# Batch 0's output products of a retention layer: one float32 matmul a head in place of three float16 ones

## The chip, the cores and the metric

The kernel runs on one core of a Trainium2 chip. The metric is the device time of one execution in microseconds (us); smaller is better. A core has a matrix engine (TensorE, PE in the profile, with its weight loads listed apart as PEld), three engines for elementwise work (VectorE or DVE, ScalarE or ACT, GpSimd or POOL), and SyncE (SP), which issues most DMAs here.

## The reference

Retention with a decay per head over blocks of tokens, then a Fourier mixing layer with an MLP, then a second MLP layer. What matters for the change is the retention, cut to its core (B = 2, H = 8 heads, S = 768 tokens, D = 64):

```python
intra = np.einsum('bhic,bhjc->bhij', qb, kb) * Dmask[None]     # masked scores
intra = np.einsum('bhij,bhjd->bhid', intra, vb)                # output products
inter = np.einsum('bhid,bhde->bhie', qb * lam_pow[None], kv_state)
out[:, :, sl] = intra + inter
kv_state = lam_block[None, :, None, None] * kv_state + np.einsum('bhsd,bhse->bhde', kb_dec, vb)
```

Behind it follow `X = fft2(x)`, `u = x + real(X)`, a layer norm, `relu(un @ w_ch1) @ w_ch2`, and the same norm and MLP once more with other weights. The reference computes in float32.

## The kernel before

**Tiling.** The kernel takes blocks of 128 tokens instead of 64, so each batch has 6 blocks (c = 0 to 5). A block of q, k or v for all 8 heads is a tile of 128 x 512 float32 (256 KB). Heads are worked in two sets, even and odd (e = 0, 1), of 4 heads each.

**Precision.** Much of the kernel splits a float32 value into a float16 pair, a high part and a remainder, and makes a product as three float16 matmuls (high by high, high by remainder, remainder by high; `PASS` in the code). In batch 0 some products multiply float32 tiles directly: scores, interstate products and the Fourier products. In the trace each float32 matmul stands as two records of a weight load and a matmul.

**One block of the retention** (batch 0), in the order in which its data flow:
- `attn_a`: GpSimd scales the keys by their decay (line 322); ScalarE and VectorE make the float16 pairs of values (lines 326, 327) and keys (lines 331, 332).
- `attn_scores` (line 346): 8 float32 matmuls, k by q, into two PSUM banks.
- `attn_x` (lines 353 to 358), once for each head set: VectorE multiplies the scores by the decay mask and a constant into `m32`, ScalarE rounds that to float16, GpSimd takes the remainder.
- `attn_o_steps` (line 426): for each of 8 heads three float16 matmuls, weights 128x128 (masked scores) and 64 moving columns (values); then VectorE adds the interstate part and writes the block to its place in `U` (lines 430, 432). For some blocks ScalarE also copies one row (lines 436 to 443).
- `attn_s_steps`: the state, 24 float16 matmuls (line 458), VectorE's sum with the decayed old state (line 465), and ScalarE's copy of it into a block-diagonal tile (line 470).
- `attn_i_steps` (line 375): the interstate product of the next block, 4 float32 matmuls from that tile, and VectorE's scaling of it (line 379).

**Order.** A scheduler orders the instructions of blocks 0 to 4 on each engine from estimated times. The end of the stage (outputs and state of block 4, all of block 5) and the Fourier stage behind it stand in an order written by hand, `ORDER`, for PE, VectorE, GpSimd and ScalarE. Its first line is

```python
c0 S B1 B0 s s B1 B0 s s O4 B1 B0 O4 c0 I O4 R I O5 O5 O5 O5 c0 c1 c2 W12 k2 j2 ...
```

where each word is the next step of a chain: S the scores of block 5, B1 and B0 the steps of `attn_x` for its two head sets, s the state of block 4, O4 and O5 outputs, I the interstate product of block 5, c0 to c2 weight conversions, W12 twelve dummy matmuls, k2 and j2 the first folds of the Fourier stage (line 489). Behind the Fourier stage come the MLPs of both layers (matmuls at lines 698, 708, 801, 848), between which the retention of batch 1 runs.

**Loads.** SyncE issues all loads of batch 0's q, k and v first, in order of blocks; tables and weights follow.

Of the kernel before, what the change touches and what calls it, by code (L numbers as in the profile page):

```python
# [15 lines left out]
ALU = mybir.AluOpType  # L16
# [16 lines left out]
QS = 64.0  # L33
MS = 256.0
# [90 lines left out]
def tile_retention_fourier_mlp(ctx: ExitStack, tc: tile.TileContext, a: dict, out: bass.AP):  # L125
    nc = tc.nc
    pe, act, dve, pool, sp = nc.tensor, nc.scalar, nc.vector, nc.gpsimd, nc.sync
# [18 lines left out]
    def bank(which, name):  # L146
        return banks[which].tile([P, 512], F32, tag=which, name=name)

    def f32t(name, spare=None):
        if spare is not None:  # L150
            return wpool.tile([P, 512], F32, tag=f"w2_{spare}", name=name)
        return fp.tile([P, 512], F32, tag="f", name=name)

    def hl(name):
        return fp.tile([P, 2, 512], F16, tag="f", name=name)
# [17 lines left out]
    loaded = {}  # L173
# [89 lines left out]
    def run(steps):  # L263
        for t in steps:
            pass
        return t
# [46 lines left out]
    vs, ks, ms = {}, {}, {}  # L313
# [34 lines left out]
    def attn_x(b, c, e, bk):  # L348
        m32 = f32t(f"m32_{b}_{c}_{e}")
        mk = mask[:, e::2]  # L350
        mk = mk[:, :, :P] if c >= 3 else mk[:, :, P:0:-1]
        mo, mi = (z.rearrange("p (h i) -> p h i", i=P) for z in (m32, pss[e]))
        dve.scalar_tensor_tensor(mo, mi, MS, mk, op0=ALU.mult, op1=ALU.mult)
        yield
        t = ms[b, c, e] = hl(f"m{b}_{c}_{e}")
        act.copy(t[:, 0], m32)
        yield
        pool.tensor_tensor(t[:, 1], m32, t[:, 0], op=ALU.subtract)  # L358
        yield

    def attn_b(b, c, bk):
        steps = [attn_x(b, c, e, bk) for e in range(2)]
        attn_scores(b, c, bk)
        for z in steps:
            next(z)
        for z in steps:
            run(z)
# [36 lines left out]
    def row_fold(b):  # L404
        y_ = row0[b]
        r = f32t(f"r{b}", 5 if b == 0 else None)
        c_ = f32t(f"rc{b}", 14 if b == 0 else None)
        pool.tensor_tensor(c_[0:1, 1:256], y_[0:1, 1:256], y_[0:1, 511:256:-1], op=ALU.add)
        pool.tensor_copy(c_[0:1, 0:257:256], y_[0:1, 0:257:256])
        pool.tensor_tensor(r[0:1, :P], c_[0:1, :P], c_[0:1, 256:128:-1], op=ALU.subtract)  # L410
        pool.tensor_tensor(r[0:1, P:ND], c_[0:1, :P + 1], c_[0:1, 256:127:-1], op=ALU.add)
        yield
        t = f32t(f"rhl{b}", 6 if b == 0 else None).bitcast(F16)[0:1].rearrange("p (two n) -> p two n", two=2)[:, :, :ND]
        act.copy(t[:, 0], r[0:1, :ND])
        yield
        pool.tensor_tensor(t[:, 1], r[0:1, :ND], t[:, 0], op=ALU.subtract)
        rhl[b] = t
        yield

    def attn_o_steps(b, c, bk):  # L420
        ps = bank(bk["o"], f"ps_o{b}_{c}")
        for h in range(H):
            (i, e), hc = divmod(h, 2), slice(h * D, (h + 1) * D)
            m_, mc = ms[b, c, e], slice(i * P, (i + 1) * P)
            for n, (x, y) in enumerate(PASS):
                pe.matmul(ps[:, hc], m_[:, x, mc], vs[b, c][:, y, hc], start=n == 0, stop=n == 2)
        yield
        x_ = U[b][c] if c < 3 else U[b][8 - c]
        if c == 0:
            dve.tensor_scalar(x_, ps, XS, None, op0=ALU.mult)  # L430
        else:
            dve.scalar_tensor_tensor(x_, ps, XS, xt[b, c], op0=ALU.mult, op1=ALU.add)
        yield
        if c == 3:
            row0[b] = f32t(f"row0{b}", 4 if b == 0 else None)
            act.copy(row0[b][0:1], x_[0:1])
            if b > 0:
                run(row_fold(b))
        elif c > 3:
            act.copy(U[b][9 - c][0:1], x_[0:1])  # L440
        yield
        if c == NCH - 1:
            act.copy(x_[0:1], row0[b][0:1])
        yield
# [28 lines left out]
    def attn_c(b, c, bk):  # L473
        run(attn_o_steps(b, c, bk))
        if c < NCH - 1:
            run(attn_s_steps(b, c, bk))
# [451 lines left out]
    def eng(n):  # L928
        return pool if n in ONPOOL.split() else dve

    wide = {}
    chains = {"s": lambda: attn_s_steps(0, 4, bk0), "O4": lambda: attn_o_steps(0, 4, bk0),
              "O5": lambda: attn_o_steps(0, 5, bk0), "I": lambda: attn_i_steps(0, 5, bk0), "R": lambda: row_fold(0)}
    for x in range(2):
        chains[f"B{x}"] = lambda x=x: attn_x(0, 5, x, bk0)
# [19 lines left out]
    with tc.manual_schedule(engines={mybir.EngineType.PE, mybir.EngineType.DVE, mybir.EngineType.Pool, mybir.EngineType.Activation}):  # L955
        for z in ORDER.split():
# [3 lines left out]
            if z[0] == "W":  # L960
                ps = bank("up", f"warm{len(warm)}")
# [145 lines left out]
```

## Time and profile before

| What | us |
|---|---|
| time, median of 3 runs | 605.07 |
| lowest and highest | 604.65, 605.29 |
| the profiled execution, its own time | 605.77 |
| span of the profiled execution | 603.9 |
| PE, busy in the span | 576.7 |
| VectorE, busy | 416.1 |
| GpSimd, busy | 280.0 |
| ScalarE, busy | 262.8 |

The profile is one execution, with the start and duration of each instruction. A busy PE isn't PE at its peak: its matmuls are pipelined and their recorded durations overlap. What a row of a pipelined burst costs is read from the whole burst and its count, not from the duration of one. Idle time of an engine is shown with what ended it. [...]

### The profile page before, as it was taken

Reading aid. Unit: us, or ns where it says so; the run is one execution under the profiler, and the core shown is the slowest. Engines: PE = TensorE matmul, PEld = TensorE weight load, DVE = VectorE, ACT = ScalarE, POOL = GpSimd, SP = SyncE. Lnnn points to the kernel's source line nnn. Section 1 sums busy time; section 2 is a strip of 40 time slices with the busy share of each in tenths; the row PEclk is TensorE's granted clock in tenths of the full one; section 3 lists DMA queues with packets and bytes.
Section 4 is the critical chain, followed back from the end, with each engine's and each line's share of the span. In section 5 each row is a group of like instructions: output and inputs, shape, how many; then the busy total and the mean of one; then the engine's idle time right before and its main releaser. Section 6 shows DMA issues by size and latency. Waiting matters only on the chain.

```text
span 603.9 us, 11882 instructions
## 1 busy us (share of the span) xinstructions
PE 576.7 (95%) x4669; PEld 379.3 (63%) x4669; DVE 416.1 (69%) x905; ACT 262.8 (44%) x530; POOL 280.0 (46%) x294
## 2 busy tenths in 40 slices
PE   6879899999999998999988999999999999999997
PEld 3756646565644554676756677666677777767773
DVE  5998799884794698886697679867544553555333
ACT  3654689654223433453457675753222222221110
POOL 7854789986253666342349665963011200020000
PEclk9899999999999999999998999999999999999999
DMA  8995259962000100443163652510110027102001
GB/s 278 396 400 187 71 176 295 304 205 69 1 1 1 35 19 9 107 130 105 46 194 111 189 162 79 158 27 1 61 28 18 2 79 63 18 1 84 22 2 52
DMA packets 46326, 63.23 MB, mean 105 GB/s; under 512 B 26176, under 2 KB 28350, under 8 KB 46270
## 3 DMA queue, kind: packets, MB, share of 16 engines
q1 hardware_dynamic: 45598, 62.40, 34.4%
q8 instruction: 36, 0.59, 0.4%
q10 hardware_dynamic: 672, 0.08, 0.1%
q14 instruction: 20, 0.16, 0.1%
HBM read 52.23 MB, written 6.29 MB: 97 GB/s over the span
## 4 chain that ended last, share of the span: by engine, by line
PE 62%; DVE 19%; ACT 7%; POOL 6%; issue 4%; DMA 1%; SPq 0%; DVEq 0%; POOLq 0%; ACTq 0%
PE ps_y L848 30%; PE ps L801 22%; PE ps_h L708 4%; DVE wf L295 2%; DVE bst L642 2%; ACT top L292 2%; DVE ps_w L294 2%; DVE tr L761 2%; PE ps_d L518 1%; POOL m L358 1%; POOL w L310 1%; PE ps_s L346 1%; PE ps_i L388 1%; POOL kd L322 1%; ACT w L308 1%
## 5 line engine op out<-in xcount | busy, mean ns | idle before, releaser
L848 PE MATMUL ps_y<-w,h 128*128 128x512 f16 x1152 | 281.9, 380 | 3.5 <-ACT h L833 1.7
L848 PEld LDWEIGHTS <-h 128*128 128x128 f16 x1152 | 109.2, 98 | 102.6 <-ACT h L833 3.8
L801 PEld LDWEIGHTS <-sw 128*128 128x128 f16 x1104 | 94.8, 98 | 23.2 <-issue 7.1
L801 PE MATMUL ps<-th,sw 128*128 128x192 f16 x828 | 92.9, 246 | 5.1 <-DVE s L814 3.6
L801 PEld LDWEIGHTS <-w 128*128 128x128 f16 x828 | 72.6, 99 | 19.1 <-issue 0.8
L310 POOL TENSOR_TENSOR w<-wf,w 128x512 f16<-128x512 f32 x58 | 67.1, 1164 | 36.3 <-ACT w L308 36.2
L833 ACT ACTIVATE h<-ps 128x384 f16<-128x384 f32 x92 | 43.8, 488 | 72.8 <-DVE ps L827 68.4
L708 PE MATMUL ps_h<-unT,w 128*128 128x384 f16 x396 | 73.7, 326 | 1.7 <-DVE h L723 1.6
L801 PE MATMUL ps<-unT,w 128*128 128x192 f16 x552 | 63.6, 248 | 0.0
L834 DVE SCALAR_TENSOR_TENSOR h<-ps,h 128x384 f16<-128x384 f32 x92 | 49.5, 554 | 14.2 <-ACT h L833 12.6
L708 PEld LDWEIGHTS <-w 128*128 128x128 f16 x396 | 36.9, 98 | 29.8 <-issue 3.1
L753 POOL TENSOR_TENSOR sw<-ws,sw 128x512 f16<-128x512 f32 x32 | 37.9, 1197 | 33.9 <-ACT sw L752 33.8
L821 DVE TENSOR_TENSOR t<-ps,s 128x192 f32<-128x192 f32 x46 | 16.3, 353 | 50.3 <-PE ps L801 50.0
L292 ACT ACTIVATE top<-ws 128x512 f16<-128x512 bf16 x57 | 44.2, 777 | 10.4 <-DVE wf L295 10.3
L813 ACT COPY s<-ps 128x192 f32<-128x192 f32 x46 | 14.5, 314 | 73.3 <-PE ps L801 73.3
L671 POOL TENSOR_TENSOR uns<-un,uns 128x512 f16<-128x512 f32 x21 | 24.6, 1171 | 43.6 <-ACT uns L670 43.4
L295 DVE TENSOR_TENSOR wf<-ps_w,top 128x512 int32<-128x512 int32 x61 | 41.3, 681 | 2.4 <-POOL w L310 1.2
L777 POOL TENSOR_TENSOR th<-ts,th 128x384 f16<-128x384 f32 x24 | 22.1, 940 | 43.2 <-ACT th L776 43.2
L308 ACT CAST w<-wf 128x512 f16<-128x512 f32 x58 | 34.9, 609 | 10.3 <-DVE wf L295 10.1
L294 DVE TENSOR_SCALAR ps_w<-ws 128x512 int32<-128x512 int32 x55 | 37.8, 689 | 0.9
L827 DVE TENSOR_TENSOR ps<-ps,s 128x192 f32<-128x192 f32 x46 | 16.6, 361 | 28.6 <-PE ps L801 28.4
L814 DVE TENSOR_TENSOR s<-ps,s 128x192 f32<-128x192 f32 x46 | 16.2, 353 | 27.7 <-ACT s L813 27.6
(161 smaller groups left out, 807.2 us busy)
## 6 DMA issues: line engine op xcount, KB each, us to landing
ws<-in_w SPq DMA_DIRECT2D x25, 511.8 KB, 4.8
ws<-in_w2b SPq DMA_DIRECT2D x16, 511.8 KB, 3.5
ws<-in_w1b SPq DMA_DIRECT2D x16, 511.8 KB, 3.6
kt<-in_kt SPq DMA_DIRECT2D x12, 256.0 KB, 4.1
qt<-in_qt SPq DMA_DIRECT2D x12, 256.0 KB, 5.6
v<-in_v SPq DMA_DIRECT2D x12, 256.0 KB
k<-in_k SPq DMA_DIRECT2D x12, 256.0 KB, 5.9
pre<-in_w SPq DMA_DIRECT2D x4, 511.8 KB
```

Of the source, the lines that this page charges most:

```text
L292: act.activation(top[:, :, 1], raw.bitcast(BF16)[:, :, 2], AF.Copy, scale=TOPS)
L294: dve.tensor_scalar(part, raw[:, :, 0], 13, None, op0=ALU.logical_shift_right)
L295: dve.tensor_tensor(ti, part, top.rearrange("p n two -> p (n two)").bitcast(I32), op=ALU.bitwise_or)
L308: act.copy(hi, t)
L310: (dve if m == 0 and i in (LD1 if kind == 1 else LD2) else pool).tensor_tensor(lo, t, hi, op=ALU.subtract)
L671: pool.tensor_tensor(s_[:, 1], un, s_[:, 0], op=ALU.subtract)
L708: pe.matmul(ps, w[:, i, k, fo:fo + P], x[:, j, k, :], start=n == 0, stop=n == 11)
L753: pool.tensor_tensor(lo, z, hi, op=ALU.subtract)
L801: pe.matmul(ps, lhs, rhs, start=start and n == 0, stop=n == 5, skip_group_check=True)
L833: act.activation(hi, z, AF.Relu)
L834: dve.scalar_tensor_tensor(lo, z, 0.0, hi, op0=ALU.max, op1=ALU.subtract)
L848: pe.matmul(dn[blk][j], h[:, x, j * P:(j + 1) * P], w[:, y], start=f == 0 and n == 0, stop=f == NF - 1 and n == 2)
```

## The change

In batch 0 the masked scores stay the float32 tile `m32`; the cast and the remainder (lines 356 and 358) aren't made, and their two steps in `ORDER` are empty. The output product of a head is one matmul of `m32` and the loaded float32 values, in place of three. The scaling of the values, which the float16 pair of the values carries, goes into the mask product's constant. The float16 pairs of values and keys are still made. Batch 1 is as before.

```diff
--- before.py
+++ after.py
@@ -350,8 +350,13 @@
         mk = mask[:, e::2]
         mk = mk[:, :, :P] if c >= 3 else mk[:, :, P:0:-1]
         mo, mi = (z.rearrange("p (h i) -> p h i", i=P) for z in (m32, pss[e]))
-        dve.scalar_tensor_tensor(mo, mi, MS, mk, op0=ALU.mult, op1=ALU.mult)
-        yield
+        dve.scalar_tensor_tensor(mo, mi, MS if b else MS * QS, mk, op0=ALU.mult, op1=ALU.mult)
+        yield
+        if b == 0:
+            ms[b, c, e] = m32
+            yield
+            yield
+            return
         t = ms[b, c, e] = hl(f"m{b}_{c}_{e}")
         act.copy(t[:, 0], m32)
         yield
@@ -422,6 +427,9 @@
         for h in range(H):
             (i, e), hc = divmod(h, 2), slice(h * D, (h + 1) * D)
             m_, mc = ms[b, c, e], slice(i * P, (i + 1) * P)
+            if b == 0:
+                pe.matmul(ps[:, hc], m_[:, mc], loaded["v", b, c][:, hc], start=True, stop=True)
+                continue
             for n, (x, y) in enumerate(PASS):
                 pe.matmul(ps[:, hc], m_[:, x, mc], vs[b, c][:, y, hc], start=n == 0, stop=n == 2)
         yield
```

## Rows read from the trace of the kernel before

**Rows 1.** The page: the span, and each engine's busy time, share and instructions.
```profile
span 603.9 us, 11882 instructions
...
PE 576.7 (95%) x4669; PEld 379.3 (63%) x4669; DVE 416.1 (69%) x905; ACT 262.8 (44%) x530; POOL 280.0 (46%) x294
```

**Rows 2.** Stretches: busy us (x count) of PE, PEld, DVE, ACT, POOL; clock, DMA share, GB/s.
```profile
20.00:30.00 10.00, 8.02 (x142) 6.81 (x138) 9.06 (x15) 6.33 (x13) 7.38 (x7) 1.00 1.04 403
30.00:40.00 10.00, 7.92 (x136) 6.80 (x136) 9.59 (x15) 5.41 (x11) 8.62 (x11) 1.00 1.02 406
...
140.00:604.00 464.00, 450.69 (x3496) 298.30 (x3494) 298.59 (x681) 173.18 (x358) 169.77 (x179) 0.99 0.23 60
```

**Rows 3.** Groups to 60 us: count, busy us, mean ns, idle before, releaser.
```profile
L358 POOL TENSOR_TENSOR m<-m,m 128x512 f16<-128x512 f32 x12 | 15.7, 1325 | 4.1 <-ACT m L356 4.1
...
L426 PE MATMUL ps_o<-vhl,m 128*128 128x64 f16 x144 | 7.3, 201 | 1.9 <-POOL m L358 1.7
...
L356 ACT CAST m<-m 128x512 f16<-128x512 f32 x12 | 7.0, 616 | 3.2 <-DVE m L353 3.2
```

**Rows 4.** Order of time, PE weight loads: start, us, engine, line, operation, count, [idle].
```profile
19.86 0.46 PEld L458 LDWEIGHTS <-khl 128*64 128x64 f16 x22
...
25.06 0.61 PEld L426 LDWEIGHTS <-m 128*128 128x128 f16 x19
25.60 0.97 PEld L375 LDWEIGHTS ps_i<-diag,qt 128*128 128x128 f32 x8
...
118.55 0.96 PEld L388 LDWEIGHTS ps_i<-state,qt 64*128 64x128 f32 x14 [0.23 <-issue]
```

**Rows 5.** PE alone by stretch: us, busy (instructions), granted clock, DMA share, GB/s.
```profile
12.00:13.00 1.00, 1.00 (x21) 0.54 1.06 389
13.00:14.00 1.00, 0.30 (x2) 0.50 1.05 387
14.00:18.00 4.00, 3.74 (x45) 0.50 1.05 387
18.00:19.00 1.00, 1.00 (x22) 0.54 1.07 387
```

**Rows 6.** Order of time, PE matmuls of the first stage.
```profile
14.58 1.20 PE L426 MATMUL ps_o<-vhl,m 128*128 128x64 f16 x19
...
27.85 1.16 PE L346 MATMUL ps_s<-qt,kt 64*128 64x128 f32 x16 [1.09 <-DVE m L353]
...
30.40 0.26 PE L426 MATMUL ps_o<-vhl,m 128*128 128x64 f16 x3 [1.22 <-POOL m L358]
...
34.76 0.73 PE L426 MATMUL ps_o<-vhl,m 128*128 128x64 f16 x19 [0.50 <-POOL m L358]
36.40 1.16 PE L375 MATMUL ps_i<-diag,qt 128*128 128x128 f32 x8 [0.90 <-ACT diag L470]
37.39 0.86 PE L426 MATMUL ps_o<-vhl,m 128*128 128x64 f16 x24
```

**Rows 7.** Order of time, VectorE up to the first fold, and one of ScalarE.
```profile
21.80 1.64 DVE L332 TENSOR_TENSOR khl<-kd,khl 128x512 f16<-128x512 f32 x1
...
25.91 0.69 DVE L327 SCALAR_TENSOR_TENSOR vhl<-v,vhl 128x512 f16<-128x512 f32 x1 [0.94 <-ACT vhl L326]
...
28.64 0.68 DVE L332 TENSOR_TENSOR khl<-kd,khl 128x512 f16<-128x512 f32 x1
...
31.04 1.53 DVE L327 SCALAR_TENSOR_TENSOR vhl<-v,vhl 128x512 f16<-128x512 f32 x1
...
33.10 1.27 DVE L353 SCALAR_TENSOR_TENSOR m<-ps_s,mask 128x512 f32<-128x512 f32 x2
...
34.89 0.41 DVE L465 TENSOR_TENSOR state<-ps_st,dec 128x256 f32<-128x256 f32 x1
...
38.99 0.68 DVE L489 TENSOR_TENSOR e<-u 128x512 f32<-128x512 f32 x1
...
35.53 0.81 ACT L470 COPY diag<-state 64x256 f32<-64x256 f32 x2
```

## The prediction

> **What bounds the kernel now.** I read the page first. TensorE is busy 95% of the span, VectorE 69%, and ScalarE and GpSimd under 50% [rows 1]. That is an average over unlike stages, so the busy times by stretch come next [rows 2]: from 140 us to the end PE is busy 450.7 of 464 us, but in the first 40 us it is not the only full engine. There the first batch's attention runs, the only place the edit touches (the scores of batch 0, lines 353 to 358, and its output products, line 426). From 20 to 40 us VectorE is busy 9.06 and 9.59 of each 10 us, PE 8.02 and 7.92. I then read the instruction groups of this stage by shape for the price of what goes [rows 3], PE's weight loads for the price of what comes [rows 4], the granted clock [rows 5], and the order of time on PE and the other engines up to the first fold [rows 6, 7]. That fold, on VectorE at 38.99 us, is my checkpoint: everything behind it (folds, Fourier products, layer norm, MLP) follows in a fixed order or from a full PE, so I carry a shift of it to the end one for one. DMA doesn't hold that point: it moves 403 and 406 GB/s from 20 to 40 us, but batch 0's q, k, v are 24 loads of 256 KB, 6.3 MB; at that rate from some 5 us on they are in near 21 us, 17 us earlier.
>
> **What is removed.** Twelve casts on ScalarE of 0.616 us and twelve subtractions on GpSimd of 1.325 us: 7.0 us and 15.7 us of busy time [rows 3]. No engine they leave is the bound of the stage, so they pay only where somebody waits for them. PE does: its two visible waits on the GpSimd result are 1.22 and 0.50 us [rows 6], and 1.7 us in all [rows 3]. A second payment is that VectorE loses time beside GpSimd. The key remainder at line 332 took 1.64 us beside two long subtractions and 0.68 us where GpSimd was idle for most of it; the value remainder at line 327 took 1.53 us beside a third, and 0.69 us before that [rows 7]. These two alone are 0.95 + 0.84 = 1.8 us. [...] VectorE's own twelve mask products stay and cost the same: only the constant changes.
>
> **What is added.** Per block, 24 float16 matmuls of 64 columns become 8 float32 ones. Each float32 matmul of this kernel stands as two records: the 4 of line 375 give 8 rows. So 24 rows become 16. What is one row worth? The 128x64 product in float32 with 128 rows of weights isn't in the trace, so I bound it. Float16 at line 426: 19 weight loads in 0.61 us, (0.61 - 0.10)/18 = 0.029 us a row [rows 4]. Float32 at line 375, the same weights with 128 columns: 8 loads in 0.97, (0.97 - 0.19)/7 = 0.112 us. Is that the weights or the 128 columns? Line 388 has 64 columns, in two halves of 64 rows that run side by side: 14 loads in 0.96, seven pairs, (0.96 - 0.19)/6 = 0.128 us a pair, with one uneven pair at the end. Half the columns, no faster: the weight load sets the pace. So I take 0.112; the lower end is the 0.056 us that line 388 gives if its halves had run one after the other. Per block 16 x 0.112 = 1.79 us against 24 x 0.029 = 0.70: **1.09 us more PE per block**, 6.5 us over six blocks (at the lower end 0.90 us a block, 0.2 more). [...]
>
> **The sum along PE.** Block 0 is nearly free: the subtraction kept PE from finishing its product until 15.8 us [rows 6], and PE was busy only 0.30 us of 13 to 14 [rows 5]. In float32 it can start behind the scores of block 1, near 12.3 us, and at the half clock of that stretch takes 2 x 1.79 = 3.6 us, to 15.9: no change. From 15.54 (interstate product of block 1) to 26.57, the last load of block 3's, PE has next to no idle, so blocks 1 and 2 add 2 x 1.09: it gets there at 28.75 instead. What is then left is scores 4 (1.16 less the 0.19 that runs on beside the next burst: 0.97), output 3 (1.79), interstate 4 (0.97), scores 5 (0.97), state 4 (22 loads took 0.46 [rows 4]: 0.5 for 24), output 4 (1.79), interstate 5 (0.97), output 5 (1.79) and a drain of 0.2: 9.95 us, to 38.70. Before, PE ended this at 37.39 + 0.86 = 38.25 after waits of 1.09, 1.22, 0.50 and 0.90 us [rows 6]; these are what pays for three times 1.09. That is +0.45. One wait stays: interstate 5 needs ScalarE's copy of state 4 (0.81 us [rows 7]), behind VectorE's last two mask products (1.27 us) and the state sum (0.41): with 0.2 from PE, 0.2 + 1.27 + 0.41 + 0.81 + gaps of 0.1 = 2.8 us after scores 5, and PE has 0.5 + 1.79 = 2.3 us of work for it. 0.5 more. **The fold starts 0.9 us later.** The GpSimd waits are gone, and PE's own weight loads are late instead. The profiled execution took 605.77 us, 1.87 over its span and 0.70 over the median of the runs, 605.07; on the profiled base the sum gives 606.7, on the median **606.0**.
>
> **The rivals.** (1) *VectorE stays the bound and gains.* If PE finds idle time for the wide products, VectorE sets the fold, without the 1.8 us of collisions and the early waits behind GpSimd (PE's gap at 13 us is one). For it: it is the fuller engine from 20 us on. Against: PE's sum above has no room. It would take a PE row of 0.056 us, or an order that moves outputs 0 and 1 into gaps before 15.5. I price it at the two collisions and half of the 1.72 us waited for GpSimd: -2.7, 602.4. [...]
> (2) *The clock returns sooner.* [...] Float32 rows of block 0 fill the gap before 14.1. If the clock returned at 15.5, the work of 3.4 us at half speed would take 1.7: 606.0 - 1.7 = 604.3. Against: from 14 to 18 us PE was busy 3.74 of 4 us and the clock still stayed at half until the end of it; I see no row that puts the return earlier.
> (3) *Outputs get in front of scores: slower.* PE takes its queue in order. An output of 1.79 us queued ahead of scores 4 or 5 delays the mask products, and with them VectorE, by that much; from the point where VectorE has no other ready work it is paid in full. With outputs 1, 2 and 3 all ahead of scores 5, and of PE's waits only the 1.09 us ahead of scores 4 won back, scores 5 come 3 x 1.09 - 1.09 = 2.2 us later, and the 0.5 us of interstate 5 comes on top: 2.7, 607.8. For it: in the trace outputs 1 and 2 stand ahead of scores 4. Against: output 3 stood behind scores 5, and before interstate 4 PE has a wait of 1.22 us to give.
>
> **How the numbers follow.** About 0.2% (1.2 us) is what a measurement of this kernel can tell from no change. Forecast, PE-bound: 0.38, its own range 604.9 to 607.4. Rival 1: 0.22. Rival 2: 0.15. Rival 3: 0.25. Faster by over 1.2 us: most of rival 1 and a third of rival 2, 0.26. Slower: most of rival 3 and a third of the forecast, 0.36. Same: 0.38. For 8 in 10 the range takes in both far rivals: 602.2 to 608.2. The order of the work behind the first stage is planned from estimates that the edit shifts, and may move a us either way; that is in the range.
>
> **What would show it.** Right: the output product's weight loads 0.11 us apart, 1.8 us a block; PE without waits between 20 and 38 us; the fold at 39.5 to 40.3; VectorE's line 332 and 327 at 0.7 us. A fold near 36 means rival 1; full clock before 18.9, rival 2; scores 4 or 5 starting later than 29 and 32.5 with VectorE idle ahead of its mask products, rival 3. A row of 0.06 us would take the ground from under the forecast, and so would a fold that moves while the end doesn't.

## The result, and the profile after

The change makes the kernel slower. Its median is 610.57 us (608.93 to 613.58, 11 executions) beside 606.07 us for the kernel before on the same chip (604.65 to 609.17, 11 executions): a ratio of 1.0082, 95% interval 1.0064 to 1.0101. The forecast was 606.0 us with a range of 602.2 to 608.2, so the time lies outside it.

The profiled execution took 613.24 us, 7.47 more than the one of before. It is one of the three slowest of the eleven, so its profile shows the loss near its largest; the medians differ by 4.5 us. The page of the kernel after, span and busy times, answers to [rows 1]:

```profile
span 611.5 us, 11759 instructions
...
PE 589.3 (96%) x4621; PEld 391.6 (64%) x4621; DVE 414.8 (68%) x905; ACT 256.6 (42%) x518; POOL 264.2 (43%) x282
```

ScalarE and GpSimd gave up 6.2 and 15.8 us, near the 7.0 and 15.7 of the removal. PE has 48 instructions fewer and 12.6 us more. Where, the stretches of the kernel after show (busy us and count of PE, PEld, DVE, ACT, POOL, then granted clock, DMA share, GB/s):

```profile
10.00:20.00 10.00, 9.87 (x87) 9.02 (x88) 6.56 (x10) 4.14 (x9) 4.47 (x5) 0.50 1.05 387
20.00:30.00 10.00, 10.00 (x75) 9.12 (x75) 5.84 (x10) 2.48 (x5) 1.87 (x3) 0.51 1.04 405
30.00:40.00 10.00, 10.00 (x115) 8.95 (x112) 7.34 (x12) 3.15 (x7) 1.32 (x2) 1.00 1.02 404
```

PE is full from 20 to 40 us, VectorE busy 5.84 and 7.34 us where it was 9.06 and 9.59 [rows 2]. The column behind the busy times is the surprise: the granted clock, as a share of the full one, is 0.51 from 20 to 30 us, where it had been 1.00. PE alone in finer stretches of the kernel after (busy, count, granted clock):

```profile
9.00:10.00 1.00, 0.59 (x2) 0.69 1.05 387
10.00:14.00 4.00, 3.96 (x23) 0.50 1.05 387
14.00:29.00 15.00, 14.91 (x129) 0.50 1.04 397
29.00:30.00 1.00, 1.00 (x13) 0.57 1.05 418
...
140.00:604.00 464.00, 454.40 (x3547) 1.00 0.23 61
```

A mean of 0.69 between 9 and 10 us puts the fall at 9.4; 0.57 between 29 and 30 puts the return at 29.9. So PE ran at half clock (granted 0.50) for 20.5 us, and before for 6.8 (12.1 to 18.9) [rows 5]. From 140 us on nothing of the change runs. What the half clock does there, and what the queue does besides, is in the order of time on PE (kernel after; start, us, line, operation, count, [idle before]); it answers to [rows 6]:

```profile
9.13 0.59 PE L346 MATMUL ps_s<-qt,kt 64*128 64x128 f32 x2 [1.45 <-DMA qt<-in_qt]
...
10.28 0.69 PE L431 MATMUL ps_o<-v,m 128*128 128x64 f32 x2
...
12.90 3.25 PE L431 MATMUL ps_o<-v,m 128*128 128x64 f32 x14
16.08 1.49 PE L466 MATMUL ps_st<-vhl,khl 128*64 128x64 f16 x46
...
18.39 2.04 PE L380 MATMUL ps_i<-diag,qt 128*128 128x128 f32 x8
...
30.28 2.00 PE L431 MATMUL ps_o<-v,m 128*128 128x64 f32 x16
```

The clock had fallen at 9.4, before the first float32 output row (10.28). Output 0 then stands in front of state 0 (the first 22 of the 46 rows at 16.08), and the interstate product of block 1 starts at 18.39. Before, it started at 15.59: state 0 had gone first, and most of output 0 had waited for GpSimd behind it (14.58 in [rows 6]). PE in the kernel before:

```profile
11.69 0.61 PE L458 MATMUL ps_st<-vhl,khl 128*64 128x64 f16 x22
...
15.59 2.06 PE L375 MATMUL ps_i<-diag,qt 128*128 128x128 f32 x8
```

Weight loads of the output product in the kernel after, at half and at full clock, as in [rows 4]:

```profile
12.90 3.06 PEld L431 LDWEIGHTS ps_o<-v,m 128*128 128x128 f32 x14 [0.23 <-issue]
...
30.28 1.86 PEld L431 LDWEIGHTS ps_o<-v,m 128*128 128x128 f32 x16
```

At full clock (1.86 - 0.19)/15 = 0.111 us a row, as forecast. At half clock it is about twice that: 14 matmul rows take 3.25 us, and 16 of them 3.68 in e13 below, 0.215 a row. VectorE up to the first fold, kernel after, as in [rows 7]:

```profile
10.62 1.53 DVE L327 SCALAR_TENSOR_TENSOR vhl<-v,vhl 128x512 f16<-128x512 f32 x1
...
16.18 0.69 DVE L438 TENSOR_SCALAR u<-ps_o 128x512 f32<-128x512 f32 x1 [3.20 <-PE ps_o L431]
16.96 0.42 DVE L471 COPY state<-ps_st 128x256 f32<-128x256 f32 x1
...
46.50 0.68 DVE L497 TENSOR_TENSOR e<-u 128x512 f32<-128x512 f32 x1
```

VectorE stands still 3.20 us for output 0. The fold comes at 46.50, 7.51 later than before, and the time is 7.47 longer: the shift went to the end one for one, as the prediction took it.

The 7.51 us can be split at the interstate product of block 1. It starts 2.80 later (18.39 against 15.59). From there to the fold after takes 28.11 us, before 23.40: 4.71 more. In this part after ran 11.5 us at half clock (18.39 to 29.9) and before 3.3 (15.59 to 18.9); 8.2 us more at half speed are 4.1 us of work, an estimate that takes all of it at half its pace, as the interstate product's 2.06 us beside 1.16 at full clock show it (kernel before, at 15.59 and 20.36). The last 0.6 is what is left for the wider rows themselves, of which the forecast had 0.9. This part of the split goes by one execution of each kernel. The others differ, by and large in step with their clock: after took 608.9 to 609.1 us at a mean clock of 0.989, and 613.2 to 613.6 at 0.979. At 0.988 the kernel before took 605.8 to 607.5 in the executions on record, and at 0.990 605.0 to 606.0. So at about one mean clock 1.4 to 4.1 us remain. The 2.80 of the queue lies within that, but no trace of those executions shows that this is what they are. Nor is the 2.80 a price that holds everywhere: in e14 below the interstate product starts as late (18.43), the clock is back by then, and the fold comes only 1.21 us later than before.

### The profile page after: what moved, and what is told of

It reads as the page before. It is cut to its first block, busy times and chain, and to the rows that moved or that the text cites. A ratio compares the mean times of both kernels' runs of the same rounds, so it can differ in the third digit from the quotient of the medians.

```text
span 611.5 us, 11759 instructions
## 1 busy us (share of the span) xinstructions
PE 589.3 (96%) x4621; PEld 391.6 (64%) x4621; DVE 414.8 (68%) x905; ACT 256.6 (42%) x518; POOL 264.2 (43%) x282
## 4 chain that ended last, share of the span: by engine, by line
PE 61%; DVE 18%; POOL 9%; ACT 8%; issue 4%; DMA 1%; DVEq 0%; ACTq 0%; POOLq 0%
PE ps_y L856 27%; PE ps L809 20%; PE ps_h L716 4%; POOL w L310 3%; PE ps_s L346 2%; PE ps_o L431 2%; DVE wf L295 2%; ACT top L292 2%; DVE bst L650 2%; DVE tr L769 1%; DVE ps_w L294 1%; PE ps_d L526 1%; ACT w L308 1%; PE ps_i L380 1%; ACT wf L307 1%
## 5 line engine op out<-in xcount | busy, mean ns | idle before, releaser
L842 DVE SCALAR_TENSOR_TENSOR h<-ps,h 128x384 f16<-128x384 f32 x92 | 49.5, 554 | 14.1 <-ACT h L841 12.6
L292 ACT ACTIVATE top<-ws 128x512 f16<-128x512 bf16 x57 | 44.3, 779 | 10.4 <-DVE wf L295 10.3
```

Source lines behind the costliest of these rows:

```text
L292: act.activation(top[:, :, 1], raw.bitcast(BF16)[:, :, 2], AF.Copy, scale=TOPS)
L842: dve.scalar_tensor_tensor(lo, z, 0.0, hi, op0=ALU.max, op1=ALU.subtract)
```

## The experiments

All are read at the same marks: the stretch at half clock in the first 45 us (its ends worked out as above), the start of the interstate product of block 1 (I1), the first fold, and over the executions the time and its mean clock (e7: nine of its ten; before: the clocks of all its executions recorded beside the others). A help for reading: an interstate product takes 1.16 us at full clock and 2.05 at half.

| kernel | half clock, us | I1 | fold | median, us | ratio to before, 95% | mean clocks |
|---|---|---|---|---|---|---|
| before | 12.1-18.9 | 15.59 | 38.99 | 606.07 | | 0.980-0.994 |
| after | 9.4-29.9 | 18.39 | 46.50 | 610.57 | 1.0082 [1.0064, 1.0101] | 0.979-0.989 |
| e1 | none | 15.73 | 38.79 | 606.18 | 0.9998 [0.9984, 1.0011] | 0.994-0.997 |
| e2 | 15.2-18.6 | 15.23 | 38.48 | 606.24 | 0.9996 [0.9982, 1.0010] | 0.992-0.994 |
| e3 | 12.0-18.9 | 15.71 | 39.98 | 607.13 | 1.0021 [1.0002, 1.0040] | 0.982-0.992 |
| e4 | 9.6-30.1 | 18.35 | 44.64 | 610.30 | 1.0067 [1.0042, 1.0091] | 0.977-0.988 |
| e5 | 10.3-20.5, 34.2-37.6 | 16.82 | 37.52 | 604.48 | 0.9965 [0.9947, 0.9983] | 0.982-0.986 |
| e6 | 16.9-37.4 | 17.43 | 50.21 | 616.99 | 1.0170 [1.0136, 1.0204] | 0.979-0.983 |
| e7 | 11.0-14.4 | 19.54 | 41.02 | 608.87 | 1.0052 [1.0023, 1.0081] | 0.980-0.994 |
| e8 | none | 14.91 | 38.56 | 605.68 | 0.9988 [0.9970, 1.0006] | 0.988-1.000 |
| e9 | 12.0-18.8 | 17.15 | 42.55 | 610.18 | 1.0067 [1.0042, 1.0092] | 0.989-0.992 |
| e10 | 9.8-30.2, 40.5-43.9 | 18.61 | 44.68 | 611.01 | 1.0079 [1.0049, 1.0108] | 0.975-0.983 |
| e11 | 15.1-18.5 | 16.84 | 42.91 | 609.21 | 1.0057 [1.0035, 1.0078] | 0.991-0.996 |
| e12 | 11.2-18.0 | 15.69 | 38.89 | 606.77 | 1.0009 [0.9988, 1.0030] | 0.986-0.992 |
| e13 | 11.5-21.7, 31.9-35.4 | 17.20 | 41.39 | 608.06 | 1.0032 [1.0012, 1.0051] | 0.982-0.989 |
| e14 | 10.8-14.2, 38.1-41.6 | 18.43 | 40.20 | 607.05 | 1.0015 [0.9998, 1.0032] | 0.988-0.994 |
| e15 | 10.3-20.6 | 17.91 | 42.08 | 609.80 | 1.0053 [1.0032, 1.0073] | 0.986-0.987 |

The mean clock takes in the whole span, with a few us at half clock near 320 us and at the end in every profiled execution. Near 320 us they last 3.4 us in most, but 6.8 in those of e1, e4, e8, e10 and e15, so the mean clock doesn't measure the first stage alone.

**e1 and e2: is it the clock?** Twelve float16 matmuls of 256 columns, whose output nobody reads, fill PE's wait of 1.45 us for the loads of block 1. e1 does so to the kernel after, e2 to the kernel before.

```diff
-                    pe.matmul(pss[e][:, t], loaded["kt", b, c][r, t], loaded["qt", b, c][r, t], start=True, stop=True)
+                    z = pe.matmul(pss[e][:, t], loaded["kt", b, c][r, t], loaded["qt", b, c][r, t], start=True, stop=True)
+        if b == 0 and c in FILL:          # FILL = {0: 12}
+            with tc.issue_after(z.ins):
+                fill = bank("up", f"fill{c}")
+                for _ in range(FILL[c]):
+                    pe.matmul(fill[:, :2 * P], ident.bitcast(F16)[:, :P], ident.bitcast(F16), start=True, stop=True)
```

> The changed kernel with twelve dummy float16 matmuls of 256 columns (some 1.3 us) behind the scores of block 0, where PE otherwise waits for the loads of block 1; the stage is otherwise the same. Theory A (clock): most of the loss is the half clock, which in the changed kernel lasted from 9.3 to 29.7 us and before from 12.1 to 18.9. If the dummies keep the clock up, the first fold comes at 38 to 40 us instead of 46.5 and the time falls to 603 to 606. Theory B (rows): the float32 weight loads bound PE at either clock; the time stays at 608 or more even with the clock up.

> The kernel before with the same twelve dummies, as control. Theory A: its half-clock stretch of 6.8 us goes or shrinks, worth at most half of it, 3.4 us, but PE waits anyway there: 603 to 605. Theory B says the same of this run, since nothing float32 is added; the two differ on the distance to the changed kernel with dummies: A under 2 us, B 3 us or more.

In the profiled execution of e1 the clock stays at 1.00 through the whole stage. PE alone, e1, and then e1's VectorE:

```profile
5.00:20.00 15.00, 12.37 (x153) 1.00 1.05 385
20.00:40.00 20.00, 19.26 (x226) 1.00 1.03 405
```

```profile
13.76 0.69 DVE L444 TENSOR_SCALAR u<-ps_o 128x512 f32<-128x512 f32 x1 [0.49 <-PE ps_o L437]
14.37 0.41 DVE L477 COPY state<-ps_st 128x256 f32<-128x256 f32 x1
...
38.79 0.68 DVE L503 TENSOR_TENSOR e<-u 128x512 f32<-128x512 f32 x1
```

Output 0 stands in front of state 0 here as well, but VectorE's wait for it is 0.49 us instead of 3.20, and the fold is back at 38.79. The change with the clock held is level with the kernel before, and so is the kernel before with the same matmuls (e2), whose clock had less to gain. So the loss of the change is a loss at half clock, the queue's part too. Both times lie a little above what was expected (606.18 for 603 to 606, 606.24 for 603 to 605), with the kernel before at 605.69 beside them; that they are within 2 us of each other is what theory A said.

**e3 and e4: which blocks?** Float32 rows only in blocks 3 to 5 (e3), or only in 0 to 2 (e4); the others keep their pairs.

```diff
-        if b == 0:
+        if b == 0 and c in WIDE:          # e3: (3, 4, 5); e4: (0, 1, 2)
             ms[b, c, e] = m32
...
-            if b == 0:
+            if b == 0 and c in WIDE:
                 pe.matmul(ps[:, hc], m_[:, mc], loaded["v", b, c][:, hc], start=True, stop=True)
```

> Float32 output products for blocks 3 to 5 of batch 0 alone; blocks 0 to 2 keep the float16 pairs. PE has the full clock there in the kernel before. Theory A: the half-clock stretch stays at some 7 us and three times 1.09 us goes into the 3.7 us that PE waited: 605 to 606.5 where the kernel before takes 605. Theory B: about half of the whole loss, 607 to 608.

> Float32 output products for blocks 0 to 2 alone. Theory A: the long half clock comes with these, so nearly the whole loss is here: 608 to 612, half clock for 13 us or more. Theory B: the other half of the loss, 607 to 608.

The late blocks cost the fold 1.0 us and leave the clock as it was. The time of e3 lies in the range of theory B (607.13 for 607 to 608), but the kernel before took 605.69 beside it, and not the 605 of the expectation; the ratio is 1.3 us, as theory A has it, and two of e3's ten executions took 610 us at a clock of 0.982. The early blocks give nearly the whole loss, with the long stretch at half clock and I1 at 18.35.

**e5: what is the removal worth by itself?** The kernel before without the remainder of the scores and without its matmul. The casts stay, and TensorE has 8 float16 rows a block less (8 x 0.029 = 0.23 us), so this isn't the removal of the change and nothing else.

```diff
         act.copy(t[:, 0], m32)
         yield
+        if b == 0:
+            yield
+            return
         pool.tensor_tensor(t[:, 1], m32, t[:, 0], op=ALU.subtract)
...
+            passes = PASS if b else PASS[:2]
```

> The kernel before, but in batch 0 the remainder of the masked scores (the GpSimd subtraction) and the one float16 matmul that uses it are left out: 16 float16 rows a block, no float32 row. It shows what the removal alone is worth. If GpSimd's collisions with VectorE and PE's waits for it count as priced, VectorE's lines 327 and 332 take 0.7 us throughout, the fold comes 1.5 to 2.7 us earlier than 39.0 and the time is 602.4 to 604. If the removal is worth nothing, 605.

VectorE in e5:

```profile
20.27 0.69 DVE L332 TENSOR_TENSOR khl<-kd,khl 128x512 f16<-128x512 f32 x1
...
28.91 0.69 DVE L327 SCALAR_TENSOR_TENSOR vhl<-v,vhl 128x512 f16<-128x512 f32 x1 [0.24 <-ACT vhl L326]
...
37.52 0.68 DVE L493 TENSOR_TENSOR e<-u 128x512 f32<-128x512 f32 x1
```

Every one of lines 327 and 332 from 10 us to the fold takes 0.68 or 0.69 us: the collisions that the prediction read in 1.64 and 1.53 [rows 7] are gone with the subtractions. The fold comes 1.5 us sooner, at the lower edge of what was expected, and the kernel gains 0.35% (2.1 us), although its clock was low for 13.7 us. It is the one variant that clearly beats both kernels, at the price of the low part of the scores.

**e6 and e7: two attempts that say less.** e6 is e1 with the casts and subtractions still made, to price the removal with the rows in place. e7 is e1 with the twelve matmuls behind the scores of block 1 (`FILL = {1: 12}`).

```diff
-            yield
-            yield
-            return
-        t = ms[b, c, e] = hl(f"m{b}_{c}_{e}")
+        t = hl(f"m{b}_{c}_{e}")
+        if b:
+            ms[b, c, e] = t
```

> The changed kernel with dummies behind the scores of block 0, and the casts and subtractions of batch 0's masked scores still made, though nobody reads them. Float32 rows without the removal, at full clock. With the changed kernel plus dummies the fold was at 38.8. If the removal is worth 1.5 to 2.7 us, the fold comes at 40.3 to 41.5 here and the time is 607 to 608.5. If PE bounds the stage by its rows, ScalarE and GpSimd's extra work costs nothing: 38.8 and 605 to 606.

> The changed kernel with the same twelve dummies one step later, behind the scores of block 1, where PE has work of its own; the wait ahead of those scores stays empty. If the wait of some 1.5 us at 8 us is what lets the clock fall, it falls here too, at some point between 9 and 12.5 us, and the time is 608 to 613. If twelve more float16 matmuls anywhere near do it, the clock stays up and the time is 606 to 607.

In e6 the added matmuls didn't hold the clock. PE alone in e6:

```profile
20.00:30.00 10.00, 10.00 (x58) 0.50 1.04 405
30.00:35.00 5.00, 5.00 (x45) 0.50 1.00 378
35.00:40.00 5.00, 5.00 (x45) 0.76 1.01 407
```

Around the fall near 16.9 PE waited 0.98 us for a cast of the keys and 0.52 for the decayed state; in e1 it waited once there, for 0.72. So e6 doesn't price the removal; it shows once more 20.5 us at half clock with PE full. e7 has seven of the twelve matmuls in front of most of output 0 on the queue and five behind state 0; nine of its ten executions spread from 607.4 to 614.9 us with clocks from 0.994 to 0.980, and the tenth took 616.7. The profiled one was low for only 3.4 us and still folded at 41.0, 2.2 later than e1, with I1 at 19.54. The place of such a filling matters, and in the middle of the dependent chain it costs.

**e8: the order behind block 0?** e1 with the outputs of blocks 0 to 3 at a lower priority for the scheduler.

```diff
-        run(attn_o_steps(b, c, bk))
+        if b == 0:
+            with tc.high_priority(offset=-150):
+                run(attn_o_steps(b, c, bk))
+        else:
+            run(attn_o_steps(b, c, bk))
```

> The changed kernel with dummies behind the scores of block 0, and the outputs of blocks 0 to 3 at lower priority, so that states and scores go ahead of them on PE. In the changed kernel output 0 stood ahead of state 0 and VectorE waited 3.2 us for it. If order is what is left of the loss (rival 3), the fold comes 1 to 3 us earlier than 38.8 and the time is 602.5 to 604.5, faster than both kernels. If PE's sum of rows sets the fold, it stays within 0.5 us of 38.8, and the time at 605 to 606.

The fold comes at 38.56, 0.2 sooner than in e1. The edit moved less than it was meant to: 12 of the 16 rows of output 0 (11.43 us) still stand in front of state 0 (12.91). So with the clock held, the order that it did change is worth next to nothing, and e8 doesn't test the order in block 0.

**e9 and e10: PE's longer sum, or float32 rows?** e9 is the kernel before with 64 float16 rows a block instead of 24 (the first product is made five times more and overwritten); e10 is e3 with `WIDE = (0,)`.

```diff
+            passes = PASS if b else PASS[:1] * 5 + PASS
```

> The kernel before, but each output group of the first batch makes its first float16 product five times more, before the three that count: 64 float16 rows a block instead of 24, 40 x 0.029 = 1.16 us more of TensorE, about what the float32 rows of the change add (1.09 us), and no float32 rows anywhere new; casts and remainders stay. If it is TensorE's longer sum in blocks 0 to 2 that keeps the clock low, half clock should last to about 28 to 30 us, the fold come at 45 to 47 us and the time be 609 to 613 us, as after the change. If it is the float32 rows themselves, the stretch at half clock should end where it did before (18.9 us, or sooner), the fold come at 39.5 to 41 us, and the time be 606 to 608 us.

> Float32 rows in block 0 alone; blocks 1 to 5 keep their float16 pairs. If the first block's float32 rows, which stand in front of state 0 at half clock, are what keeps the clock low, it should stay low past 25 us and the time be 609 to 612 us, as with blocks 0 to 2. If it takes float32 rows through the whole stretch, the clock should be back by 19 to 22 us, and the time be 605.5 to 607.5 us (one block of 1.09 us, half of it at half clock: fold at 39 to 41 us).

PE alone in e9, and the same in e10:

```profile
12.00:18.00 6.00, 5.73 (x87) 0.50 1.05 387
18.00:19.00 1.00, 1.00 (x6) 0.60 1.07 387
```

```profile
10.00:16.00 6.00, 5.74 (x32) 0.50 1.04 385
16.00:30.00 14.00, 13.90 (x144) 0.50 1.04 399
30.00:31.00 1.00, 1.00 (x37) 0.88 0.99 393
```

e9 has about the PE time of the change and gets its clock back at 18.8, where it was before. e10 has float32 output rows in one block of six, none after 16.4 us, and is at half clock until 30.2 with PE busy 13.90 of the 14 us to 30. That one block gives as large a loss as the whole change (1.0079 beside 1.0082), at mean clocks that are lower still. e9 is slow for another reason: the chain of work that ended last in e9 runs through the remainders, which still have to be made:

```profile
35.12 2.29 POOL m L358 x2
37.41 0.05 issue
37.45 1.60 PE ps_o L427 x49
```

So my time for e9 was missed (610.2 instead of 606 to 608), though its clock did what the second theory expects.

**e11: the removal at one clock.** e9 with the filling of e1: what e6 was meant for.

> e9 with e1's twelve float16 products of 256 columns behind the scores of block 0: TensorE has as long a sum as after the change, the casts and remainders are still made, and the clock should be held at full through the first 40 us, as in e1. Against e1 (606.18 us, fold at 38.79) it prices the removal alone at one clock. If the removal only gives VectorE its 1.5 us back (e5), the fold should come at 40 to 40.5 us and the time be 607 to 608 us. If the casts and remainders stand in the chain between VectorE's masked scores and TensorE's longer output rows, as e9's chain shows for block 5, the fold should come at 41.5 to 42.5 us and the time be 608.5 to 610 us. If the added products do not hold the clock here, as in e6, it says nothing of the removal.

The filling didn't hold the clock throughout: it was at half from 15.1 to 18.5. The fold comes at 42.91, 4.1 later than e1's and 0.4 past the range of the second theory; 3.4 us at half clock can account for 1.7 of that. Over the executions at a mean clock of 0.994, e11 took 608.8 to 610.2 us and e1 606.2 to 607.2: beside about as long a PE sum, the casts and remainders cost some 2.5 to 3 us. In e11 GpSimd makes the last four remainders from 35.48 to 40.03, and PE waits for them in the last output products.

**e12: only block 0?** e3 with `WIDE = (1, 2)`.

> Float32 rows in blocks 1 and 2 alone; blocks 0 and 3 to 5 keep their float16 pairs. If it is the float32 rows in the first block at half clock that delay the clock's return, the stretch at half clock should end by 19 to 22 us and the time be 606 to 608 us. If any float32 rows before the clock has returned delay it, the stretch should last past 25 us and the time be 609 to 612 us, as with block 0 alone.

The order of time on PE in e10 and then in e12, around block 0:

```profile
13.13 3.25 PE L432 MATMUL ps_o<-v,m 128*128 128x64 f32 x14
16.31 1.49 PE L467 MATMUL ps_st<-vhl,khl 128*64 128x64 f16 x46
...
18.61 2.05 PE L381 MATMUL ps_i<-diag,qt 128*128 128x128 f32 x8
```

```profile
14.68 1.19 PE L435 MATMUL ps_o<-vhl,m 128*128 128x64 f16 x19 [0.15 <-POOL m L364]
15.69 2.06 PE L381 MATMUL ps_i<-diag,qt 128*128 128x128 f32 x8
...
19.74 1.77 PE L432 MATMUL ps_o<-v,m 128*128 128x64 f32 x14
```

With the pairs kept in block 0, I1 starts at 15.69, the clock is back at 18.0, and the wide rows of blocks 1 and 2 cost nothing: fold at 38.89, ratio 1.0009. So the loss comes with block 0.

**e13, e14 and e15: its rows or its place?** e13 is e10 with output 0 behind state 0 on PE's queue. e14 keeps the early place without float32 rows: the kernel before with no subtraction in block 0 and 64 float16 rows in its output (the high part made six times more and overwritten, the remainder left out). e15 is the whole change with output 0 behind state 0.

```diff
+        if b == 0 and c == 0:             # e13, e15
+            run(attn_s_steps(b, c, bk))
+            with tc.issue_after(last[b, c].ins):
+                run(attn_o_steps(b, c, bk))
+            return
...
+            passes = PASS[:1] * 6 + PASS[:2] if first else PASS     # e14
```

> As e10 (float32 rows in block 0 alone), but on TensorE's queue block 0's output product stands behind the 24 rows of state 0. If the order does it, interstate 1 starts near 15.6 to 16.5 us instead of 18.6, the half clock ends by 19 to 22 us, and the time is 605.5 to 607.5 us, as in e12. If the float32 rows themselves keep the clock low, the stretch still lasts past 25 us, and of e10's loss only the 2 to 3 us of the order come back: 607.5 to 609.5 us.

> The kernel before, but block 0 has no subtraction on GpSimd, and its output groups make the product with the high parts six times more (the first six are overwritten) and leave out that with the remainder: 64 float16 rows, 64 x 0.029 = 1.86 us, ready early and ahead of most of state 0 on the queue, like the float32 rows of e10 (1.79 us). The low part of block 0's scores is left out. If the order and the early start do it, the clock stays low past 25 us or interstate 1 starts near 18 us, and the time is 608 to 611 us. If the float32 rows do it, the half clock ends by 19 to 22 us, and only the place costs: 606 to 608.5 us.

> The whole change (float32 rows in all six blocks), with block 0's output product behind the 24 rows of state 0 on TensorE's queue. If the order does it, the change becomes neutral as with the clock held (e1, e8): interstate 1 near 16 us, half clock over by 22 us, the fold at 39 to 40.5 us, the time 605.5 to 607.5 us. If the float32 rows keep the clock low, half clock lasts past 25 us, the fold comes at 43 to 45 us, and the time is 608 to 611 us.

PE in e13, and then in e14:

```profile
11.58 0.85 PE L467 MATMUL ps_st<-vhl,khl 128*64 128x64 f16 x22
12.36 3.68 PE L432 MATMUL ps_o<-v,m 128*128 128x64 f32 x16
...
17.20 2.08 PE L381 MATMUL ps_i<-diag,qt 128*128 128x128 f32 x8
```

```profile
13.05 2.33 PE L431 MATMUL ps_o<-vhl,m 128*128 128x64 f16 x56
15.31 0.85 PE L463 MATMUL ps_st<-vhl,khl 128*64 128x64 f16 x39
...
18.43 1.16 PE L378 MATMUL ps_i<-diag,qt 128*128 128x128 f32 x8
```

e14 has its output in the early place, in front of most of state 0, and pays for the place: I1 at 18.43. But it is at full clock by 14.2 (the interstate product takes 1.16), its clocks are 0.988 to 0.994, and it loses 0.15%, with an interval that reaches zero. e13 has the float32 rows in the later place: I1 at 17.20 is still late, since the 3.68 us of rows come in front of it, half clock 13.6 us in two stretches, clocks 0.982 to 0.989, ratio 1.0032. It lies between e10 and e12: its time, 608.06, is what the theory of the rows expected, its clock, back at 21.7, what the theory of the order did. e15 has a ratio of 1.0053, between e13 and the change, and is as divided: half clock over at 20.6, but I1 at 17.91, the fold at 42.08 and 609.80 us. Neither theory holds alone. Float32 rows in block 0 in the early place go with a lower clock (median of the mean clocks 0.977 in e10, 0.981 in e4, 0.986 in after), and the same PE time in float16 rows doesn't (0.990 in e9, 0.991 in e14; the kernel before had 0.989 beside e13 to e15). In the later place the clock is only a little lower (0.985 in e13, 0.986 in e15), within the range of the kernel before. The place seems to cost besides, since e13 lies under e10 and e15 under after, but the intervals of both pairs overlap. How the two join isn't settled: e5, with no float32 output row, was at half clock for 13.7 us too, the kernel before has executions at 0.980, and e13 and e15 had half the stretch of e10 and after.

## Why the prediction was wrong, point by point

- **What bounds the kernel, and the checkpoint: right.** The fold's shift came out at the end within 0.5 us in after (7.51 against 7.47) and in ten of the fifteen experiments. In e1, e4, e8, e10 and e15 the end came 0.7 to 1.6 us later than the fold says; these are the executions with 6.8 instead of 3.4 us at half clock near 320 us, a term that the prediction doesn't have. No load held the fold.
- **What is removed: right in the main, and undervalued in words.** ScalarE and GpSimd lost about what the rows said, and the collisions ended with the subtractions (e5). "They pay only where somebody waits for them": they pay 1.5 us at the fold in e5, and some 2.5 to 3 beside long output products (e11 against e1). In the sum this stood as PE's waits for GpSimd, 1.72 us, and the rest of 3.7 us of waits to be won back. In e5, without the subtractions, lines 327 and 332 took 0.68 and 0.69 us; in after line 327 took 1.53 and 1.06 once each and line 332 1.10, beside other GpSimd instructions (lines 322 and 459). One row was misread: where line 332 took 0.68 us, at 28.64, GpSimd was not idle. Its subtraction ran at the same time and took 1.69 us, where another took 1.15 (at 13.38, kernel before), so such a meeting seems to cost GpSimd as well:

```profile
28.65 1.69 POOL L358 TENSOR_TENSOR m<-m,m 128x512 f16<-128x512 f32 x1 [2.62 <-ACT m L356]
```

- **What is added: right.** 0.112 us a row was forecast, 0.111 measured, at full clock; PE became the bound, without a wait between 20 and 40 us.
- **The sum along PE: this step failed, at "Block 0 is nearly free".** Its arithmetic held: output 0 was to end at 15.9, and VectorE could take it at 16.18. The conclusion "no change" didn't follow. I let the sum go on "from 15.54", the interstate product of block 1, without asking what stood behind output 0 on PE's queue. It was state 0, from which that product comes: with output 0 in front it starts at 18.39, and 2.80 us are lost before block 1. The order isn't all of it: in e13, with state 0 in front, output 0 ends near 16.0 as forecast, but 1.2 us of scores and state rows, part of which had run in PE's gaps before, still come between it and that product (17.20; in e15 17.91). The rest of the sum then took the clock of the kernel before, full from 18.9 on, as given. In the profiled execution it came back at 29.9, which is 4.1 us more. Why it came back so late stays open; the runs show that it came with float32 rows in block 0 (e10) and not with the same rows in blocks 1 and 2 (e12) or as much float16 work (e9, e14), and that the loss is gone where the clock never falls (e1). What I summed from there on, +0.9, is at the upper end of what the runs show once the clock is held or block 0 left alone: 39.98 for wide rows in the late blocks (e3, +1.0), 38.79 for all (e1, -0.2), 38.89 for blocks 1 and 2 (e12, -0.1). Of the 4.6 us by which the time of 610.57 lies over the forecast, 1.0 is the base: the 605.07 was a median of three executions, that of eleven is 606.07.
- **Rival 1, VectorE gains: no.** PE had no room. Without wide rows the gain is real (e5): 1.5 us at the fold and 2.1 by the ratio, where I priced 2.7.
- **Rival 2, the clock: the right quantity with the wrong sign.** I asked whether float32 rows in the gap near 13 us would bring the clock back sooner, found no row for it, and didn't ask whether it could come later. Its 3.4 us were 18.9 [rows 5] less a return at 15.5, which was my estimate; with float32 rows in block 0 the clock came back at 29.9 (after), 30.2 (e10) and, with them behind state 0, 21.7 (e13) and 20.6 (e15). A rival with the half clock reaching to 30 us would have been priced at 11/2 = 5.5 us, and would have put the range past 611.
- **Rival 3, outputs in front of what the chain needs: the right mechanism in the wrong block.** I placed it at blocks 1 to 4, where rows at full clock and PE's waits could pay for it; it happened in block 0, where a row costs about twice as much (0.215 us at half clock, 0.111 at full) and the state of block 0 waits behind it.

## What to carry to other kernels

Before calling an operation free because it starts earlier, list what stands behind it on its engine's queue; a wait that held it back may have let the critical chain pass. Where a stretch at half clock lies beside the change, take its length as one of the unknowns, in both directions, and read it in several executions: here eleven executions of the kernel after spread from 608.9 to 613.6 us, in step with their mean clock. And convert the late parts of a chain rather than its start: wide rows in blocks 1 and 2 cost nothing here, in blocks 3 to 5 1.0 us at the fold, and in block 0 alone the whole loss.

## What the hardware did that I had not expected

TensorE stayed at half clock (granted 0.50) with next to no idle time: from 14 to 29 us it was busy 14.91 of 15 us in the kernel after, from 16 to 30 us 13.90 of 14 in e10, where after 16.4 us the same kinds of rows ran as in the kernel before. What kept it low in these 14 us no run shows. The fall at 9.4 us comes at a wait of TensorE, of 1.45 us for a load (to 9.13), but the kernel before has the same wait (1.45 us, to 9.36) and fell only at 12.1, and in the 20.5 us after the fall the longest wait is 0.32 us.

With twelve matmuls in that wait (1.48 us) the granted clock was 1.00 from 5 to 45 us in the profiled executions of e1 and e8. It wasn't in e2 and e11, which were at half from 15 to 18.6 us, nor in e6, where PE waited again later (0.98 and 0.52 us) and the clock was at half from 16.9 to 37.4. And a float32 row of this kernel, one of the two records that each float32 matmul leaves, cost 0.111 us at full clock with 64 moving columns, and 0.22 at half.
